# Biased attention with a feed-forward layer on one Trainium2 core: the first head pair's bias band is made on the chip, and the first eight pairs are laid in a new order

## The chip, the cores and the metric

The kernel runs on one core of a Trainium2 chip. The core has TensorE (matrix products into PSUM), VectorE, ScalarE (exponentials, copies), GpSimd and SyncE, each with an instruction queue of its own that runs in order, and 16 DMA engines that move data between HBM and SBUF. The metric is the device time of one execution in microseconds (us); less is better.

In the rows of the profile PE is TensorE, PEld its weight loads, DVE VectorE, ACT ScalarE, POOL GpSimd and SP SyncE; a "q" behind a name is that engine's instruction queue. `<-` stands between what is written and what is read, and a bracket at the end of a row gives how long the engine had been idle and what ended that. L354 is line 354 of the kernel.

## The reference

Eight batches of eight heads, 576 positions, 64 numbers a head. The bias depends on the distance of two positions through a table of 32 rows, and all distances of 128 or more share its last row.

```python
scores = scale * np.matmul(q, k.transpose(0, 1, 3, 2))        # q, k, v: (8, 8, 576, 64)
n = np.abs(pos[:, None] - pos[None, :])
bucket = np.where(n < 16, n, large)                           # large: by the logarithm of n, at most 31
scores = scores + bias_table[bucket].transpose(2, 0, 1)[None] # bias_table: (32, 8)
attn = np.exp(scores - np.max(scores, axis=-1, keepdims=True))
attn = attn / (np.sum(attn, axis=-1, keepdims=True) + 1e-09)
x = np.matmul(attn, v).transpose(0, 2, 1, 3).reshape(4608, 512)
h = x @ w_in                                                  # w_in: (512, 2048)
out = np.maximum(0.01 * h, h) @ w_out                         # w_out: (2048, 512)
```

## The kernel before, in words

**Pairs.** Two heads of a batch make a pair, one on SBUF partitions 0 to 63 and one on 64 to 127: 32 pairs, four to a batch. Keys are cut into chunks of 128, and scores are made transposed (keys on partitions, queries along the row). For pair n the steps are named by short words:

- `tq n`, `tk n`: TensorE transposes the loaded queries or keys into PSUM (line 292 up to pair 5, 288 for pairs 6 to 8; later pairs by DMA). `cq n a` or `cq n v` copies the queries to SBUF on ScalarE or VectorE (L307), `ck n` the keys on VectorE (L313), and `ap n` (L299) lays out the last 64 keys.
- `m n u`: TensorE makes score unit u. Units 0 to 3 are a chunk of 128 keys by 512 queries for both heads (L354); unit 4 is the last 64 queries of all four chunks (L347); unit 5 is the last 64 keys (L357, L358). Each takes one of two score buffers in PSUM (tag `ps_s`); unit 4 takes the banks `o0` and `o1` in the plain form and a score buffer with `s`.
- `e n u`: ScalarE takes the exponential of that unit into SBUF (L373 for units 0 to 3, L375 or L380 for unit 4, L385 for unit 5).
- `b n u`: VectorE multiplies the part of the unit near the diagonal by the bias band (L408; L401 for unit 5 of pair 0, in two halves). The bias is applied as a factor exp(bias - last bias), which is 1 at distances of 128 or more, so only a band is touched.
- `at n`, `ac n e c`: TensorE multiplies by the values and a column of ones: the last keys (L421), then chunk c for head e (L432), into banks `o0` and `o1`. `h0 n` and `h1 n` do the same in two phases with two half-height matmuls side by side (L476).
- `dv n e`: VectorE divides by the sums (L452, L454). `xt n`, `xc n`: TensorE transposes the result and VectorE copies it into `xT` (L490, L496). From pair 6 a transposing DMA does this (`xt6`), but for pair 7.

**Feed-forward.** Tokens are cut into tiles of 512. An input piece makes 128 of the 2048 hidden rows of a tile with four matmuls (L532); `l` applies the leaky function on ScalarE (L556) or, `l 1`, on VectorE (L551, L554). An output piece (`o`) has four matmuls (L584). Tile 0 can begin when all four pairs of batch 0 are in `xT` (`fin 3`); `p0` and `p1` make a piece's first three and last matmuls apart. `i m`, `i s`, `i o0`, `i o1` are input pieces in a bank of the given tag, `moe` one with its leaky function. `rows n` and `turn n` arrange later pairs for transposing DMAs (L270, L278), `sl` and `begin` issue loads.

**The order.** Pairs 0 to 7 are written out by hand in one long string `first`, a list of these steps; each step puts its instructions behind what its engines already have. From pair 8 on loops lay out the rest, and TensorE works on scores, values and feed-forward pieces by turns. `spin k` issues k products of ones whose result nobody reads (L1020): `o` in bank `o0`, `m` in a bank of the transposes.

**The bias band.** `ub` holds, for each of the eight heads on a partition of its own, the factor by signed distance in a row of 512. A band needs, on partition r, that row shifted by r. So `ub` is written to a row tensor `u_row` in HBM (L202), and `load_hk` reads it back with a stride of one element from partition to partition into `hk` (128 partitions, head, 384): the value at (r, head, x) is `u_row[head, r + x]`. `load_hk4` does the same for the last keys (L211). All are issued on SyncE's queue in this order:

```python
nc.sync.dma_start(out=udr.ap(), in_=ub)
load_hk(0, 2); load_hk(2, 4); load_hk4(0, n_pairs); load_hk(4, 6); load_hk(6, H)
```

Loads of queries, keys, values and weights are issued on GpSimd's queue (L124, L131, L137, L144, L246, L250).

## Time and profile before

| What | Value |
|---|---|
| Median of 3 runs | 365.95 us (365.65 to 367.32) |
| The profiled execution | 367.74 us, span of the profile 366.0 us |
| TensorE busy | 358.4 us (98%) |
| ScalarE busy | 244.1 us (67%) |
| VectorE busy | 189.3 us (52%) |
| First exponential of pair 0 | starts at 7.11 us |
| First band of pair 0 | starts at 12.98 us |
| First input product | starts at 32.60 us |
| First score of pair 8 | starts at 64.27 us |

A share of busy time is a mean over the span. The first 65 us, which the hand-written order covers, are unlike the rest: there the engines fill up one after another. The busy time of a matmul includes a modelled end that overlaps with the next one, so rows that group several matmuls give the better cost of one.

### The profile page before, as it was taken

The page shows a single profiled execution, that of the slowest core. Times are in us where ns is not written, and L with a number is a line of the kernel's source. Part 1 is how long each engine was busy: PE and PEld are TensorE (multiplying, and loading weights), DVE is VectorE, ACT ScalarE, POOL GpSimd, SP SyncE. Part 2 cuts the span into 40 slices and gives each one's busy share as a digit, 9 for nine tenths or more (in the row PEclk, how much of TensorE's full clock was granted, in tenths as well). Part 3 has the DMA queues.
Part 4 walks back from the last instruction along what each step waited for, and adds up shares of the span by engine and source line. Part 5 has one row for each costly group of instructions (what it writes and reads, how often), then busy time and mean ns, then how long its engine had stood idle before and what let it go on. Part 6 is the DMA issues. An engine that isn't in the chain of part 4 may idle for free.

```text
span 366.0 us, 11897 instructions
## 1 busy us (share of the span) xinstructions
PE 358.4 (98%) x5099; PEld 212.2 (58%) x5099; DVE 189.3 (52%) x499; ACT 244.1 (67%) x363; POOL 105.4 (29%) x195
## 2 busy tenths in 40 slices
PE   6999999999999999999999999999999999999996
PEld 2466555555556777686666666666666544444443
DVE  3498777877766667565666555566554300200000
ACT  5699987568957888777777777777777264055111
POOL 8867417242253433433343334211000000000000
PEclk9699999999999999999999999999999999999999
DMA  8999999999888998997997779965111000200212
GB/s 101 192 193 155 192 205 137 176 150 145 99 103 142 118 142 125 154 123 100 136 130 120 122 119 129 131 111 95 51 48 50 30 29 0 87 29 0 85 60 86
DMA packets 105851, 40.26 MB, mean 110 GB/s; under 512 B 83648, under 2 KB 101320, under 8 KB 105800
## 3 DMA queue, kind: packets, MB, share of 16 engines
q0 software_dynamic: 55200, 18.36, 48.0%
q1 hardware_dynamic: 49304, 19.06, 26.5%
q10 hardware_dynamic: 1296, 2.10, 1.6%
q8 instruction: 40, 0.66, 0.8%
q14 instruction: 11, 0.09, 0.1%
HBM read 37.68 MB, written 9.45 MB: 129 GB/s over the span
## 4 chain that ended last, share of the span: by engine, by line
PE 90%; DVE 4%; ACT 2%; DMA 1%; issue 1%; POOL 1%; ACTq 0%; POOLq 0%
PE pm L822 34%; PE pm L584 16%; PE pm L532 15%; PE ps_o L476 7%; PE ps_s L354 7%; DMA kn<-in_k_dram 1%; PE pm L718 1%; DVE at L408 1%; ACT at L373 1%; PE ps_o L421 1%; PE ps_o L442 1%; PE ps_o L432 1%; PE ps_s L822 1%; PE pm L577 1%; PE ps_s L347 1%
## 5 line engine op out<-in xcount | busy, mean ns | idle before, releaser
L373 ACT ACTIVATE at<-ps_s 128x1024 bf16<-128x1024 f32 x120 | 118.7, 1022 | 35.4 <-PE ps_s L354 34.5
L822 PE MATMUL pm<-xT,w_in_sb 64*128 64x512 bf16 x608 | 139.7, 376 | 0.0
L822 PE MATMUL pm<-w_out_sb,gt 64*128 64x512 bf16 x544 | 129.7, 376 | 0.0
L556 ACT ACTIVATE gt<-pm 128x512 bf16<-128x512 f32 x140 | 82.4, 602 | 40.0 <-PE pm L532 34.4
L408 DVE TENSOR_TENSOR at<-at,hk 128x768 bf16<-128x768 bf16 (+3 forms) x149 | 64.7, 451 | 30.8 <-ACT at L385 20.8
L822 PEld LDWEIGHTS <-w_in_sb 64*128 64x128 bf16 x608 | 51.9, 94 | 23.0 <-issue 1.2
L532 PE MATMUL pm<-xT,w_in_sb 128*128 128x512 bf16 x268 | 61.5, 379 | 0.0
L584 PE MATMUL pm<-w_out_sb,gt 128*128 128x512 bf16 x268 | 59.8, 379 | 0.0
L822 PEld LDWEIGHTS <-gt 64*128 64x128 bf16 x544 | 48.2, 94 | 19.0 <-issue 0.7
L354 PE MATMUL ps_s<-qt,kt 64*128 64x512 bf16 x240 | 45.2, 385 | 0.5 <-ACT at L373 0.2
L584 PEld LDWEIGHTS <-gt 128*128 128x128 bf16 x268 | 25.6, 98 | 30.2 <-DMA vn<-in_v_dram 0.4
L532 PEld LDWEIGHTS <-w_in_sb 128*128 128x128 bf16 x268 | 25.0, 98 | 28.1
L131 POOL DMA_DIRECT2D vn<-in_v_dram x32 | 33.6, 1054 | 9.2 <-PE pm L822 4.9
L476 PEld LDWEIGHTS <-at 64*128 64x128 bf16 x1760 | 33.8, 94 | 3.4 <-issue 0.5
L476 PE MATMUL ps_o<-vn,at 64*128 64x65 bf16 x1760 | 35.6, 190 | 0.0
L385 ACT ACTIVATE at<-ps_s 128x576 bf16<-128x576 f32 x30 | 19.7, 658 | 18.0 <-PE pm L822 18.0
L454 DVE TENSOR_TENSOR opair<-ps_o,rcp 128x320 bf16<-128x320 f32 x64 | 29.2, 487 | 1.7 <-issue 0.4
L873 DVE COPY y<-pm 128x512 f32<-128x512 f32 x17 | 11.8, 691 | 27.6 <-PE pm L822 27.6
L597 DVE COPY y<-pm 128x512 f32<-128x512 f32 x11 | 7.6, 691 | 34.1 <-PE pm L584 34.0
L1064 POOL COPY tick<-opair 1x1 bf16<-1x1 bf16 x43 | 7.8, 182 | 58.9 <-DVE opair L454 58.9
L1064 POOL COPY tick<-at 1x1 bf16<-1x1 bf16 x21 | 4.8, 227 | 58.3 <-DVE at L408 55.9
L124 POOL DMA_DIRECT2D kn<-in_k_dram x30 | 19.3, 644 | 7.0 <-issue 6.6
(106 smaller groups left out, 343.6 us busy)
## 6 DMA issues: line engine op xcount, KB each, us to landing
out_dram<-y SPq DMA_DIRECT2D x28, 256.0 KB, 3.5
qn<-in_q_dram POOLq DMA_DIRECT2D x28, 144.0 KB, 4.5
kn<-in_k_dram POOLq DMA_DIRECT2D x28, 144.0 KB, 3.8
vn<-in_v_dram POOLq DMA_DIRECT2D x24, 128.0 KB, 4.5
w_in_sb<-in_moe_w_in_dram POOLq DMA_DIRECT2D x4, 512.0 KB, 8.7
w_out_sb<-in_moe_w_out_dram POOLq DMA_DIRECT2D x2, 1024.0 KB, 14.1
...
```

Source lines behind the costliest of these rows:

```text
L124: nc.gpsimd.dma_start(out=dst[0:RQ, h0:h1, :, :].rearrange("r h c d -> r h (c d)"), in_=src[b, h0:h1, :, :].rearrange("h (r c) d -> r h (c ...
L131: nc.gpsimd.dma_start(out=vn[b % NBUF][:, c, h0:h1, 0:D], in_=v[b, h0:h1, c * P : (c + 1) * P, :].rearrange("h s d -> s h d"),)
L354: nc.tensor.matmul(ps[:, e, :], lhsT=kt[r, u * P : (u + 1) * P], rhs=qt[r, 0:512], start=True, stop=True)
L373: nc.scalar.activation(at[:, :, u, 0:512], ps, AF.Exp, scale=scale)
L385: nc.scalar.activation(at4[:, 0:w], ps.rearrange("p e i -> p (e i)")[:, 0:w], AF.Exp, scale=scale)
L408: nc.vector.tensor_tensor(out=o, in0=o, in1=m, op=ALU.mult)
L454: nc.vector.tensor_tensor(out=opair[:, 0:m, e * D : (e + 1) * D], in0=ps[:, :, 0:D], in1=rcp.to_broadcast([P, m, D]), op=ALU.mult)
L476: m = nc.tensor.matmul(outs[n][e][:, ic * (D + 1) : (ic + 1) * (D + 1)], lhsT=at[halves[r], o : o + P], rhs=vn[b % NBUF][halves[r], c, 2 * ...
L532: nc.tensor.matmul(pm, lhsT=w_in_sb[:, c, f * P : (f + 1) * P], rhs=xT[c][:, T * TT : (T + 1) * TT], start=(c == 0), stop=(c == n_cc - 1))
L556: nc.scalar.activation(g, pm, AF.Prelu, bias=0.0, scale=1.0, alpha=0.01)
L584: nc.tensor.matmul(pm, lhsT=gt[:, f, ts * P : (ts + 1) * P], rhs=w_out_sb[:, f, :], start=(f == 0), stop=(f == n_fc - 1))
L822: m = nc.tensor.matmul(o, lhsT=w, rhs=x, start=was is None, stop=need[bank] == 0)
```

## The change

The band of heads 0 and 1 is no longer read from `u_row`; `load_hk(0, 2)` goes, while `u_row` and the other reads stay. In its place:

- `place`, a row of zeros with two ones for each head, made on VectorE, gives one-hot weights. `dm` (`windows`) is 12 products that put 12 windows of `ub`, each 159 long and 32 apart, of both heads on 24 partitions of one PSUM bank. `dc` (`windows_copy`) copies them to SBUF as `wins` on ScalarE.
- `hm` (`slants`) is 32 transposes: number j takes columns j to j + 127 of `wins` (24 x 128) and writes 24 columns of 128 partitions, so that each partition gets its shift. `hc e` (`slants_copy`) copies head e's 384 columns into `hk` on VectorE, putting window i, shift j at column 32 i + j.

The string `first` is laid anew. Ten of 17 spins go (9, 2, 3 and 3 become one group of 7). `m 0 1` comes ahead of `tq 1`; `m 0 4` and `m 3 4` use `o0` and `o1`, `m 1 4` a score buffer; pair 3's values go in two halves; `cq 5` and `cq 6` go to VectorE and `cq 7` to ScalarE; bands, values and feed-forward pieces of pairs 0 to 7 stand in another order. There are as many input (16) and output (4) pieces as before. The step `ii` is defined and not used.

```diff
--- before.py
+++ after.py
@@ -206,6 +206,37 @@
             in_=bass.AP(tensor=udr, offset=h0 * UW, ap=[[1, P], [UW, h1 - h0], [1, BW]]),
         )
 
+    NB0 = BW // 32
+    place = per.tile([H, 2 * NB0 + NB0 - 1], BF16, name="place")
+    nc.vector.memset(place, 0.0)
+    for e in range(2):
+        c = e * NB0 + NB0 - 1
+        nc.vector.tensor_copy(out=place[:, c : c + 1], in_=ident[0:H, e : e + 1])
+    wins = per.tile([2 * NB0, 32 + P], BF16, name="wins")
+    near = {}
+
+    def windows():
+        near["w"] = ps_o_pool.tile([P, 512], FP32, name="ps_d", tag="o1")
+        for i in range(NB0):
+            nc.tensor.matmul(near["w"][0 : 2 * NB0, 0 : 31 + P],
+                             lhsT=place[:, NB0 - 1 - i : 3 * NB0 - 1 - i], rhs=ub[:, 32 * i : 32 * i + 31 + P],
+                             start=(i == 0), stop=(i == NB0 - 1))
+
+    def windows_copy(eng):
+        copy = nc.scalar.copy if eng == "a" else nc.vector.tensor_copy
+        copy(out=wins[:, 0 : 31 + P], in_=near.pop("w")[0 : 2 * NB0, 0 : 31 + P])
+
+    def slants():
+        near["h"] = ps_o_pool.tile([P, 8 * P], BF16, name="ps_h", tag="o1")
+        for j in range(32):
+            nc.tensor.transpose(near["h"][:, j * 2 * NB0 : (j + 1) * 2 * NB0], in_=wins[:, j : j + P],
+                                identity=ident[0 : 2 * NB0, 0 : 2 * NB0])
+
+    def slants_copy(e, eng):
+        copy = nc.scalar.copy if eng == "a" else nc.vector.tensor_copy
+        copy(out=hk[:, e, :].rearrange("p (i j) -> p j i", j=32),
+             in_=near["h"][:, 0 : 64 * NB0].rearrange("p (j e i) -> p e j i", e=2, i=NB0)[:, e])
+
     def load_hk4(p0, p1):
         for e in range(2):
             nc.sync.dma_start(
@@ -214,7 +245,6 @@
                             ap=[[1, SL], [2 * UW, p1 - p0], [1, P + SL]]),
             )
 
-    load_hk(0, 2)
     load_hk(2, 4)
     load_hk4(0, n_pairs)
     load_hk(4, 6)
@@ -1089,35 +1119,35 @@
         exp(n, u, qk_mm(n, u))
 
     first = """
-        spin 9 o, tq 0, cq 0 a, tk 0, ck 0, ap 0, spin 2 o,
-        begin 0, m 0 0, m 0 2, tk 1, tq 1, e 0 0, m 0 1, ck 1, e 0 2, m 0 5, e 0 1, e 0 5, m 0 4 s, m 0 3,
-        e 0 4, spin 3 m, cq 1 v, ap 1, e 0 3, m 1 0, tk 2, b 0 5, ck 2, b 0 1, e 1 0, m 1 1, ap 2, m 1 2,
-        e 1 1, b 0 0, b 0 4, m 1 4, tq 2,
-        begin 1, e 1 4, spin 3 m, m 1 3, b 0 2, e 1 2, b 1 0, cq 2 v, at 0, ac 0 1 0, ac 0 1 1, ac 0 0 0,
-        b 1 1, ac 0 1 2, m 1 5, e 1 3, ac 0 1 3, ac 0 0 1, e 1 5, ac 0 0 2, ac 0 0 3, m 2 0, e 2 0, tk 3,
-        b 1 4, dv 0 0, m 2 1, b 1 5, tq 3, e 2 1, dv 0 1, m 2 3, ck 3, at 1, e 2 3, ac 1 0 0, m 2 2, b 1 2,
-        cq 3 v,
-        begin 2, ac 1 0 1, ac 1 1 0, m 2 5, ac 1 1 1, b 2 0, ac 1 1 2, e 2 2, ac 1 1 3, ac 1 0 2, ac 1 0 3,
-        e 2 5, ap 3, b 2 1, m 3 0, dv 1 0, xt 0, m 2 4 s, b 2 5, xc 0, e 3 0, dv 1 1, tk 4, m 3 2, e 2 4,
-        m 3 1, ck 4, b 2 4,
-        begin 3, at 2, e 3 2, ac 2 0 0, b 2 2, ac 2 0 1, ac 2 1 0, e 3 1, xt 1, b 3 0, m 3 3, tq 4,
-        ac 2 0 2, xc 1, ac 2 0 3, dv 2 0, ac 2 1 1, ac 2 1 2, e 3 3, ac 2 1 3, m 3 5, dv 2 1, cq 4 a,
-        e 3 5, ap 4, tq 5, m 3 4 s, xt 2, m 4 0, e 3 4, b 3 1, e 4 0, m 4 1, e 4 1, b 3 5,
-        begin 4, b 3 4, at 3, ac 3 1 0, ac 3 0 0, b 3 2, xc 2, ac 3 0 1, cq 5 a, ac 3 1 1, ac 3 0 2,
-        ac 3 0 3, ac 3 1 2, fin 3, ac 3 1 3, p0 0, m 4 2, e 4 2, m 4 3, dv 3 0.1, b 4 1, e 4 3, xt 3 o0,
-        p0 1, xc 3, b 4 0, p1 0 0, m 4 4 s, p1 1 0, m 4 5, tk 5, rows 6, e 4 5, e 4 4, moe, ck 5, b 4 5,
-        ap 5, moe, tq 6, m 5 0, b 4 4, cq 6 a, at 4, m 5 1, e 5 1, ac 4 1 0, ac 4 1 1, ac 4 0 0, ac 4 0 1,
-        begin 5, e 5 0, b 4 2, ac 4 0 2, ac 4 0 3, ac 4 1 2, dv 4 0, tk 6, ac 4 1 3, m 5 5, e 5 5, dv 4 1,
-        sl 5 1, i m, m 5 2, ck 6, b 5 0, l 0, m 5 3, b 5 1, m 5 4, i m, e 5 2, e 5 3, xt 4, i s, l 1,
-        rows 7, e 5 4, xc 4, i s, b 5 5, l 0, sl 5 2, b 5 4,
-        begin 6, i m, at 5, ap 6, l 0, b 5 2, m 6 0, l 0, m 6 1, tk 7, ac 5 0 0, ac 5 1 0, ck 7, ac 5 1 1,
-        ac 5 0 1, ac 5 0 2, ac 5 0 3, ac 5 1 2, tq 7, e 6 1, e 6 0, dv 5 0, ac 5 1 3, dv 5 1, sl 6 1, i s,
-        l 0, m 6 2, xt 5, m 6 3, e 6 2, cq 7 v, b 6 0, e 6 3, xc 5, m 6 4, ap 7, i m, m 6 5, e 6 4, i m,
-        l 0, l 1, i o0, i m, e 6 5, m 7 0, m 7 1, l 0, b 6 5, b 6 1, sl 6 2, at 6, l 0, b 6 2, b 6 4,
-        begin 7, rows 8, ac 6 1 0, ac 6 1 1, e 7 0, ac 6 0 0, ac 6 0 1, ac 6 0 2, e 7 1, ac 6 1 2,
-        ac 6 0 3, ac 6 1 3, tk 8, dv 6 0, dv 6 1, sl 7 1, ck 8, i s, i m, l 0, m 7 4, l 0, m 7 2, xt6,
-        m 7 3, b 7 0, e 7 4, o, e 7 3, turn 7, b 7 1, o, e 7 2, b 7 4, m 7 5, tq 8, cq 8 a, b 7 2, o,
-        e 7 5, b 7 5, ap 8, sl 7 2, o,
+        spin 7 o, tq 0, tk 0, ck 0, cq 0 a,
+        begin 0, ap 0, dm, m 0 0, m 0 2, dc a, hm, hc 0 v, tk 1, hc 1 v, e 0 0, e 0 2, m 0 1, e 0 1, tq 1,
+        ck 1, m 0 5, m 0 4, cq 1 v, e 0 5, e 0 4, m 0 3, tk 2, e 0 3, ck 2, ap 1, m 1 4 s, tq 2, b 0 1,
+        e 1 4, m 1 0, b 0 2, e 1 0, m 1 1,
+        begin 1, b 0 4, e 1 1, b 0 5, m 1 2, ap 2, m 1 3, cq 2 v, b 0 0, e 1 2, at 0, e 1 3, ac 0 1 0,
+        b 1 0, ac 0 1 1, ac 0 0 0, m 1 5, b 1 2, ac 0 0 1, e 1 5, ac 0 0 2, ac 0 1 2, ac 0 1 3, b 1 1,
+        ac 0 0 3, m 2 0, m 2 1, dv 0 0, e 2 0, tk 3, m 2 3, b 1 5, b 1 4, dv 0 1, tq 3, at 1, ck 3,
+        ac 1 0 0, e 2 1, m 2 5, ac 1 0 1,
+        begin 2, ac 1 1 0, b 2 1, ac 1 1 1, e 2 3, ap 3, m 2 2, cq 3 v, ac 1 1 2, e 2 5, ac 1 1 3, e 2 2,
+        b 2 5, ac 1 0 2, ac 1 0 3, b 2 0, dv 1 0, m 3 0, dv 1 1, xt 0, e 3 0, xc 0, m 2 4 s, tk 4, m 3 2,
+        e 2 4,
+        begin 3, b 2 2, at 2, b 2 4, m 3 1, xt 1, ac 2 0 0, ac 2 0 1, ck 4, ac 2 1 0, e 3 2, e 3 1, b 3 2,
+        ac 2 0 2, m 3 3, ac 2 1 1, xc 1, ap 4, ac 2 0 3, tq 4, ac 2 1 2, dv 2 0, e 3 3, cq 4 a, ac 2 1 3,
+        dv 2 1, m 3 5, e 3 5, tq 5, m 3 4, b 3 1, e 3 4, m 4 1, xt 2, b 3 5, at 3, m 4 0, b 3 0, e 4 1,
+        e 4 0,
+        begin 4, b 3 4, cq 5 v, xc 2, fin 3, b 4 0, h0 3, m 4 2, e 4 2, h1 3, m 4 3, e 4 3, dv 3 0.1, p0 0,
+        m 4 4 s, xt 3 o0, b 4 1, p0 1, xc 3, m 4 5, rows 6, p1 0 0, p1 1 0, i o0, e 4 5, tk 5, ck 5, i m,
+        ap 5, l 0, e 4 4, b 4 5, tq 6, m 5 1, m 5 0, at 4, b 4 2, b 4 4, ac 4 1 0, cq 6 v, l 0,
+        begin 5, ac 4 0 0, ac 4 0 1, ac 4 0 2, ac 4 0 3, e 5 0, ac 4 1 1, dv 4 0, tk 6, ac 4 1 2, e 5 1,
+        ac 4 1 3, m 5 5, e 5 5, dv 4 1, i m, l 0, m 5 2, m 5 3, e 5 2, ck 6, m 5 4, sl 5 1, e 5 4, e 5 3,
+        i m, b 5 5, l 0, xt 4, b 5 0, ap 6, rows 7, xc 4, i s, b 5 2, i o1, i m, sl 5 2, m 6 1, b 5 4, l 0,
+        begin 6, m 6 0, b 5 1, l 0, l 0, at 5, ac 5 0 0, e 6 1, ac 5 0 1, tk 7, e 6 0, ac 5 1 0, ac 5 0 2,
+        tq 7, cq 7 a, ac 5 0 3, ac 5 1 1, ac 5 1 2, dv 5 0, ac 5 1 3, dv 5 1, sl 6 1, i s, l 0, m 6 2,
+        ck 7, ap 7, b 6 1, m 6 4, xt 5, m 6 3, e 6 2, xc 5, i m, e 6 3, m 6 5, e 6 4, e 6 5, i m, b 6 2,
+        i o0, l 1, b 6 5, i m, b 6 4, m 7 1, b 6 0, l 0, at 6, m 7 0, rows 8, sl 6 2, l 0,
+        begin 7, l 0, e 7 0, ac 6 1 0, ac 6 0 0, ac 6 0 1, ac 6 0 2, b 7 0, ac 6 1 1, tk 8, i m, ac 6 0 3,
+        ac 6 1 2, ac 6 1 3, e 7 1, ck 8, i m, m 7 2, dv 6 0, l 0, e 7 2, m 7 3, dv 6 1, m 7 4, l 1, ap 8,
+        sl 7 1, e 7 3, o, turn 7, b 7 1, b 7 2, m 7 5, e 7 5, e 7 4, o, b 7 4, o, b 7 5, sl 7 2, tq 8,
+        cq 8 a, xt6, o,
     """
 
     def word(w):
@@ -1159,6 +1189,23 @@
             if f == 0: gts[T] = gt_pool.tile([P, n_fc, TT], BF16, name="gt")
             in_steps(pm, T, f, range(n_cc))
             open_.append((T, f, pm))
+        elif k == "dm": windows()
+        elif k == "dc": windows_copy(a[0])
+        elif k == "hm": slants()
+        elif k == "hc": slants_copy(a[0], a[1])
...
         elif k == "l": leaky(*open_.pop(0), a[0])
         elif k == "o": piece_out()
         else: raise ValueError(k)
```

13 lines of the change are left out of this document (added).

## The prediction, written before the result was known

> **What bounds the kernel now.** I read the shares of the page first, then the busy time by stretches, then the timeline of the first 37 us row by row, then the landing times of single transfers.
>
> ```profile
> PE 358.4 (98%) x5099; PEld 212.2 (58%) x5099; DVE 189.3 (52%) x499; ACT 244.1 (67%) x363; POOL 105.4 (29%) x195
> ...
> 20.00:25.00 5.00, 4.83 (x91) 3.09 (x89) 4.89 (x14) 4.78 (x7) 2.84 (x6) 1.00 1.65 187
> 25.00:30.00 5.00, 4.72 (x117) 3.46 (x115) 4.56 (x14) 4.96 (x7) 2.67 (x4) 1.00 1.59 186
> ...
> 35.00:40.00 5.00, 4.86 (x66) 2.71 (x66) 3.03 (x8) 4.66 (x9) 2.98 (x5) 1.00 1.38 189
> ...
> 100.00:200.00 100.00, 100.00 (x1854) 69.09 (x1852) 63.35 (x166) 76.47 (x110) 39.12 (x76) 1.00 0.91 126
> ```
>
> TensorE is busy 98% of the span and all of 100 to 200 us, so from some point on a microsecond is worth a microsecond of TensorE work. The change can gain only where TensorE is not yet full. Between 20 and 30 us TensorE looks busy too (4.83 and 4.72 of 5), but a matmul's busy time holds its modelled end; ScalarE (4.78, 4.96) and VectorE (4.89, 4.56) are what is full there. So there is a first stage, set by exponentials and bands, and a second, set by TensorE. These rows give both ends of the first:
>
> ```profile
> 6.14 0.61 PE L1020 MATMUL ps_w<-const-bfloat16-1.0 128*128 128x512 bf16 x2
> 7.11 1.94 ACT L373 ACTIVATE at<-ps_s 128x1024 bf16<-128x1024 f32 x2 [1.03 <-PE ps_s L354]
> 8.34 0.92 SPq L204 DMA_DIRECT2D hk<-u_row  x2
> 9.23 0.50 PEld L292 LDWEIGHTS <-kn 96*64 96x64 bf16 x12 [2.00 <-DMA kn<-in_k_dram]
> 9.95 0.76 DVE L313 COPY kt<-ps_t 128x576 bf16<-128x576 bf16 x1 [2.62 <-PE ps_t L292]
> 10.97 1.02 ACT L373 ACTIVATE at<-ps_s 128x1024 bf16<-128x1024 f32 x1 [1.93 <-PE ps_s L354]
> 12.98 0.52 DVE L401 TENSOR_TENSOR at<-at,hk 64x192 bf16<-64x192 bf16 x2 [1.48 <-DMA hk<-u_row]
> 13.13 1.46 PE L1020 MATMUL ps_w<-const-bfloat16-1.0 128*128 128x512 bf16 x3
> 13.24 1.02 ACT L373 ACTIVATE at<-ps_s 128x1024 bf16<-128x1024 f32 x1 [0.16 <-PE ps_s L354]
> 15.18 2.15 ACT L373 ACTIVATE at<-ps_s 128x1024 bf16<-128x1024 f32 x2 [0.92 <-PE ps_s L354]
> 15.81 0.76 DVE L313 COPY gt<-ps_t 128x576 bf16<-128x576 bf16 x1 [2.31 <-PE ps_t L292]
> ...
> 20.31 3.77 ACT L373 ACTIVATE gt<-ps_s 128x1024 bf16<-128x1024 f32 x4
> ...
> 30.18 0.60 ACT L375 ACTIVATE at<-ps_s 128x512 bf16<-128x512 f32 x1
> 30.28 1.59 DVE L408 TENSOR_TENSOR at<-at,hk 128x768 bf16<-128x768 bf16 x4
> 31.36 1.40 PE L432 MATMUL ps_o<-vn,at 128*128 128x65 bf16 x40
> 32.60 0.81 PE L532 MATMUL pm<-xT,w_in_sb 128*128 128x512 bf16 x3
> ...
> 36.30 0.45 PE L292 MATMUL ps_t<-ident,kn 96*64 96x96 bf16 x12
> 36.79 1.89 PE L532 MATMUL pm<-xT,w_in_sb 128*128 128x512 bf16 x8
> 64.27 0.39 PE L354 MATMUL ps_s<-qt,kt 64*128 64x512 bf16 x2
> ```
>
> ```profile
> 31.27 0.15 PE ps_o L421 x10
> ...
> 44.23 2.59 PE pm L532 x12
> ```
>
> The first exponential (`e 0 0`) starts at 7.11, the last of pair 3 (`e 3 4`) ends at 30.18 + 0.60 = 30.78. From 20.31 on ScalarE has no gap worth counting; before that it idles 1.93 + 0.16 + 0.92 = 3.01 us, each time for scores. The first of these, 1.93, is `m 0 1`, which stands behind `tk 1` and `tq 1` in TensorE's order, and `tk 1` waits for pair 1's keys (the row at 9.23, 2.00 idle, released by that transfer). The bias band is waited for once, 1.48 us, by VectorE at 12.98; then VectorE waits 2.31 us more for `tk 2`, which stands behind three spins and a score. The input product starts at 32.60. `tk 5` starts at 36.30, and pair 8's first score at 64.27.
>
> After 36.30 the work of TensorE up to 64.27 is, by the order: 14 input and 4 output pieces of 4 matmuls (0.86 each: the two rows are of the chain of waits, 2.59 for 12 matmuls and 0.15 for a pair's tails), 3 pairs of values with tails (1.4 + 0.15), 12 scores at 0.22, six smaller ones 1.15, 5 transposed halves and `xt` twice, 1.9: 15.5 + 4.6 + 2.6 + 1.2 + 1.9 = 25.8 of 28.0 us. So 2.2 us are stalls; the rest only moves with its start.
>
> **The change part by part.** *Spins.* Ten of 17 go (0.43 to 0.2 us each). All stood where TensorE had nothing else ready, and no work waits on their result: 0, except that the clock may miss them (rival B).
>
> ```profile
> 17.23 0.65 ACT L380 ACTIVATE at<-ps_q 128x256 bf16<-128x256 f32 x2
> ...
> DMA to landing us min/median/max: 4.5/4.5/4.5
> ...
> L476 PE MATMUL ps_o<-vn,at 64*128 64x65 bf16 x1760 | 35.6, 190 | 0.0
> L385 ACT ACTIVATE at<-ps_s 128x576 bf16<-128x576 f32 x30 | 19.7, 658 | 18.0 <-PE pm L822 18.0
> ```
>
> These are a copy of 2 x 256 columns, the time to landing of the band's read issued at 8.34, and the page's groups of the small matmuls on values and of the narrow exponentials (mean ns last before the bar).
>
> *The products (`dm`) and their copy (`dc`).* Twelve products of 159 columns and 8 rows stand before `m 0 0`, where two spins of 512 columns stood (6.14). Nothing like them is in the trace. Lower bound: the 65-column matmuls of 31.36, 1.40 / 40 = 0.035 each, 0.4 us. Upper: a full spin, 0.61 / 2, 3.7 us. I take the spin scaled by columns, 0.22 x 159 / 512 = 0.067, so 0.8 us, because 159 columns is nearer to the narrow rows; against the two spins' 0.43 that is 0.37 later. `dc` reads 24 x 159 on ScalarE ahead of `e 0 0`; the first row gives 0.65 / 2 for 256 columns, so at most 0.33, and it runs while `m 0 0` runs. Bounds 0 and 0.33; I take 0. `e 0 0` then starts near 7.45: cost 0.35.
>
> *The transposes (`hm`).* 32, each a weight load of 128 columns and 24 moving columns. Lower bound 0.035 each as at 31.36: 1.1 us. Upper bound the 0.19 us that its group has as one matmul's whole duration, if nothing overlaps: 6.1 us. I take 1.1: weight loads of the same width, narrower moving side. They fit between `m 0 2` (ended about 7.5) and 9.2, where pair 1's keys land, so TensorE's idle 1.7 us covers them. Without that cover they would cost their 1.1 us in full. The new wait: `hm` waits for `dc`, and behind it in TensorE's queue stand `tk 1` and `m 0 1`.
>
> *The two copies (`hc`) on VectorE.* 128 x 384 from PSUM with a stride each; the copy at 9.95 takes 0.76 for 576 columns, so 0.5 each (bounds 0.4 and 0.76). VectorE idles 2.62 us until 9.95. `hm` ends near 8.6, so the copies end at 9.65; `ck 1` is ready at the same time. Cost 0, and each further tenth delays `ck 1`, `cq 1` and pair 1. `place` (a memset and two one-column copies) falls in VectorE's pause before the first key copy: 0.
>
> *The band through HBM.* Of six reads of `u_row`, the first (192 KB) goes; the write and the other five stay. SyncE's queue reaches pair 1's read about 0.5 us sooner. Pair 1's keys were issued ahead of all this and keep their 9.2. The gain is on VectorE: pair 0's band is in SBUF at 9.65 instead of 8.34 + 4.5 = 12.8.
>
> *The new order, first stage.* `m 0 1` stands right behind `tk 1`: keys at 9.2, transposes 0.3 and scores 0.4 later, so `e 0 1` at 9.95 instead of 10.97. From there I walked the three queues with two score banks: `e 0 5` 10.95 (0.66 by its group), `e 0 4` (now in two halves, +0.05) 11.6, `e 0 3` 12.25, `e 1 4` 13.2, `e 1 0` 13.8, then every 0.95 up to `e 1 3`, `e 1 5` to 18.25. ScalarE idles 0.5 before `e 0 1`, 0.2 before `e 2 0`, and I allow 0.3 elsewhere: 1.0 instead of 3.01. `e 3 4` ends at 30.78 + 0.35 + 0.05 - 2.0 = 29.2. VectorE must keep up: from its band at 16.60 in the old order to the last of pair 3 at 30.28 + 1.59 = 31.87 it is busy nearly throughout, 15.3 us. The same work plus the two half bands of pair 0 (0.5) begins at 12.6 in the new order (`tk 2` no longer waits behind spins), so 28.4 without gaps; I find one of 0.5 for `e 1 2` and others together as long, 29.4, and the last band follows `e 3 4` at 29.2 + 0.45. Bands end about 29.7, 2.1 us ahead.
>
> Transfers have to be there too. The tightest are the keys of pair 3 (issued first here), pair 4 and pair 8, each with the largest time to landing:
>
> ```profile
> 11.23 0.64 POOL L124 DMA_DIRECT2D kn<-in_k_dram  x1 [0.30 <-DMA kn<-in_k_dram]
> DMA to landing us min/median/max: 7.8/7.8/7.8
> ...
> 12.54 0.67 POOL L124 DMA_DIRECT2D kn<-in_k_dram  x1
> DMA to landing us min/median/max: 8.7/9.3/9.9
> ...
> 39.45 0.67 POOL L124 DMA_DIRECT2D kn<-in_k_dram  x1
> DMA to landing us min/median/max: 11.1/12.2/13.3
> ```
>
> 11.23 + 7.8 = 19.0, where `tk 3` comes at 18.7; 12.54 + 9.9 = 22.4, needed at 23.5; and 39.45 + 13.3 = 52.75 for `rows 8`, which stood after 56: slack for a lead of 3 us. Cost 0, with the 0.3 at `tk 3` hidden behind `e 2 0`.
>
> ```profile
> 64.66 0.78 PE L476 MATMUL ps_o<-vn,at 64*128 64x65 bf16 x40
> ```
>
> *Values of pair 3 in halves* (`h0`, `h1`): 80 matmuls, by this row 2 x 0.6, its end left out, against 1.35 at 31.36: gain 0.1. `m 4 2` and `m 4 3` (0.44) now stand ahead of the input product, where TensorE would have waited for bands.
>
> *Second stage.* ScalarE loses `cq 5` and `cq 6` and takes `cq 7`; VectorE the reverse, 0.7 us each, with 3.03 of 5 busy there: hidden; if VectorE were full it would cost 0.7. By my walk the first-stage work plus `m 4 5` and the second input piece ends at 34.5; in the old order at 36.3, where `tk 5` follows it. The lead is 1.8. Then an input piece follows at once, where before TensorE went from `tk 5` at 36.30 to the next piece at 36.79, 0.2 more than the transposes need: 0.3 more of lead with the gap ahead of `tk 5`. The later order has the same 25.8 us of work; which of its 2.2 us of stalls stay I cannot tell, so 0, between -0.7 and +0.7. `xt6`, a transposing transfer, goes behind pair 9's on SyncE's queue instead of ahead of it; its rows are wanted only with pair 7's: 0.
>
> **Sum:** +0.35 (products) +0.05 (two halves) -2.0 (ScalarE's idle) -0.4 (`cq 5` off ScalarE, halves, earlier scores) -0.3 (piece behind `tk 5`) +0.2 (VectorE's gaps) = -2.1. The profiled execution took 367.74, span 366.0 and 1.7 round it; it would be 365.6. The runs' median, 365.95, is 1.8 below that execution: 363.85, say 363.9.
>
> **The rivals.** *A, the forecast:* 363.9, by itself 362.6 to 364.8 (stall term, and ScalarE's idle between 0.7 and 1.5). Chance 0.58.
>
> ```profile
> 9.00:10.00 1.00, 0.77 (x20) 0.77 (x22) 0.05 (x1) 0.05 (x1) 0.78 (x2) 0.64 2.00 139
> 10.00:11.00 1.00, 1.00 (x13) 0.44 (x10) 1.00 (x2) 0.03 (x1) 0.86 (x2) 0.50 1.16 117
> ...
> 16.00:17.00 1.00, 1.00 (x24) 0.59 (x21) 0.97 (x2) 0.89 (x2) 0.65 (x1) 0.95 1.26 248
> ```
>
> *B, the clock falls and costs part of it.* The granted clock was 0.64 at 9 to 10 us, 0.50 until 16, 0.95 in 16 to 17. It fell after 1.7 idle us, and came back after spins that now are gone. For: the 32 transposes use 24 of 128 rows, and may count for little. Against: by the durations above TensorE is occupied in 2.3 of the 3.1 us from 6.1 to 9.2. At the low clock scores for `e 0 1` come 0.5 later, and if it lasts to pair 0's values (1.4 us) half of that again is lost: 0.5 to 1.5, so 364.9. [...] Chance 0.16.
>
> *C, the change doesn't do what it says:* the band was hidden anyway. For: only VectorE waited for it, 1.48 us, and 2.31 us for `tk 2` right after. Then the order alone decides, and if VectorE's gaps in pairs 1 to 3 are 2 us instead of 1, and stalls after 36 grow by 0.7, 0.3 is left: 365.6. Chance 0.16.
>
> *D, slower:* the transposes do not overlap, 0.19 us each. `hm` then ends at 7.5 + 6.1 = 13.6 with `tk 1` and `m 0 1` behind it, so `e 0 1` starts 4.4 later than in A: 363.9 + 4.4 = 368.3. It decides from 0.115 us a transpose (1.7 of cover + 2.0 of lead, over 32). For: they read their windows at odd offsets, as no load in the trace does. Against: 40 loads as wide took 1.40. Chance 0.10.
>
> **How the numbers follow.** 0.5% is 1.8 us, about what a measurement of this kernel can tell. A gives faster with 0.47 and within with 0.11; B and C within; D slower, 0.10. So faster 0.47, same 0.43, slower 0.10. The range 362.6 to 366.3 takes in A, B and C and leaves out D and the edges.
>
> **What the profile after would show.** Right: `e 0 1` near 10, pair 0's first band near 12.6, `e 3 4` ending near 29.2, the input product near 31.5, pair 8's first score near 62. `hm` taking over 1.7 us, a clock of 0.5 past 13 us, or VectorE idle over 1.5 us in 13 to 30, would show the step that failed. A lead at 34 us that is gone at pair 8 would put it on the later order.

## The result: 0.7% slower

The changed kernel takes 368.01 us (367.84 to 369.85, 7 runs) against 365.93 for the kernel before in the same session, a ratio of 1.0068, 95% interval 1.0046 to 1.0089: 2.1 us slower, where the prediction had 363.9 and 362.6 to 366.3. Executions of one kernel differ by up to 1.2% here (a_warm below: 366.13 to 370.41), and the three profiles of the kernel before differ in their clock (at half rate for 10.2, 6.8 and 3.4 us in executions of 368.8, 367.74 and 366.43), so each profile below stands beside its own execution's time. Those of the changed kernel make two groups, 367.8 to 368.1 and 369.2 to 369.9 (six and eight of the 14 in two sessions). So the 2.1 us are the loss of the first group; the median of the second session is 369.2, and the loss of the second group about 3.3. The first profile of the changed kernel is of one of 369.35 us; another, of 368.07 and so of the first group, is read here (a_again below). Its timeline (start, duration, engine, line, operation, and in brackets the idle time before it and what ended it):

```profile
4.77 0.45 PE L322 MATMUL ps_t<-ident,qn 96*64 96x96 bf16 x12 [0.98 <-DMA qn<-in_q_dram]
5.54 0.45 PE L322 MATMUL ps_t<-ident,kn 96*64 96x96 bf16 x12 [0.33 <-DMA kn<-in_k_dram]
5.92 1.00 PE L221 MATMUL ps_d<-ub,place 8*24 8x159 bf16 x12
6.95 0.28 ACT L227 CAST wins<-ps_d 24x159 bf16<-24x159 f32 x1 [1.06 <-PE ps_d L221]
7.46 1.94 ACT L403 ACTIVATE at<-ps_s 128x1024 bf16<-128x1024 f32 x2 [0.22 <-PE ps_s L384]
7.78 1.03 PE L232 MATMUL ps_h<-ident,wins 24*128 24x24 bf16 x32
8.85 3.50 DVE L237 COPY hk<-ps_h 128x384 bf16<-128x384 bf16 x2 [1.74 <-PE ps_h L232]
10.02 1.02 ACT L403 ACTIVATE at<-ps_s 128x1024 bf16<-128x1024 f32 x1 [0.62 <-PE ps_s L384]
11.99 0.94 DVE L343 COPY kt<-ps_t 128x576 bf16<-128x576 bf16 x1
12.41 0.39 PE L377 MATMUL ps_q<-qt,kt 64*128 64x64 bf16 x7 [1.05 <-DVE hk L237]
21.27 2.86 ACT L403 ACTIVATE gt<-ps_s 128x1024 bf16<-128x1024 f32 x3 [0.90 <-PE ps_s L384]
34.29 0.82 PE L562 MATMUL pm<-xT,w_in_sb 128*128 128x512 bf16 x2
64.61 0.39 PE L384 MATMUL ps_s<-qt,kt 64*128 64x512 bf16 x2
```

TensorE is still busy 97% of the span (356.8 us), against 98% before. `dm` (L221) took 1.00, `dc` (L227) 0.28, `hm` (L232) 1.03, the first exponential (L403) starts at 7.46, `e 0 1` at 10.02: all near the forecast. The two band copies (L237) took 3.50 us, 1.75 each. They hold PSUM bank `o1`, so `m 0 4` (L377) waits for them (TensorE 1.05 us, the row at 12.41), and `ck 1` (L343) stands behind them until 11.99. Pair 2's first exponential is at 21.27, the first input product (L562) at 34.29, pair 8's first score (L384) at 64.61.

The kernel before, profiled again in an execution of 366.43 us (b_again2), near its median:

```profile
6.77 2.96 ACT L373 ACTIVATE at<-ps_s 128x1024 bf16<-128x1024 f32 x3 [1.03 <-PE ps_s L354]
7.65 0.45 PE L292 MATMUL ps_t<-ident,kn 96*64 96x96 bf16 x12 [0.47 <-DMA kn<-in_k_dram]
12.36 0.52 DVE L401 TENSOR_TENSOR at<-at,hk 64x192 bf16<-64x192 bf16 x2 [2.67 <-DMA hk<-u_row]
13.23 0.76 DVE L313 COPY gt<-ps_t 128x576 bf16<-128x576 bf16 x1 [0.35 <-PE ps_t L292]
17.96 1.02 ACT L373 ACTIVATE gt<-ps_s 128x1024 bf16<-128x1024 f32 x1 [0.24 <-PE ps_s L354]
30.73 0.81 PE L532 MATMUL pm<-xT,w_in_sb 128*128 128x512 bf16 x2
62.41 0.39 PE L354 MATMUL ps_s<-qt,kt 64*128 64x512 bf16 x2
```

Pair 8's first score (L354 in this kernel's lines) is at 62.41, not at the 64.27 of the profile that the prediction read. The three first exponentials run without a gap from 6.77: pair 1's keys were there at 7.65, not at 9.23, and the 1.93 us in which ScalarE waited for them do not exist. The changed kernel is 64.61 - 62.41 = 2.2 us behind at this point, where the measured loss is 2.1 and these two executions differ by 1.6. From there on the two spans have 302.3 (before) and 301.7 us left. So the whole loss of this execution is made before pair 8.

One place where it can be made is the granted clock. Columns of the next two are the stretch (us), its length and TensorE's busy time (matmuls), the granted clock, the share of the DMA engines and GB/s; first the changed kernel (a_again), then before (b_again2):

```profile
5.50:7.00 1.50, 1.46 (x26) 0.98 1.07 153
7.00:8.90 1.90, 1.90 (x40) 0.50 1.38 179
8.90:12.30 3.40, 2.45 (x29) 0.50 1.39 144
12.30:16.00 3.70, 3.36 (x45) 0.50 1.35 188
16.00:20.00 4.00, 3.24 (x41) 0.50 1.36 212
```

```profile
5.50:7.00 1.50, 1.44 (x18) 1.00 1.24 173
7.00:8.90 1.90, 1.34 (x29) 1.00 1.33 171
8.90:12.30 3.40, 2.31 (x16) 0.78 1.32 168
12.30:16.00 3.70, 3.70 (x55) 0.75 1.36 208
```

TensorE of the changed kernel was occupied for all but 0.04 us of 5.5 to 8.9, but it was at half rate from 6.9 until 20.6 us. Ahead of that, behind its seven spins, it had stood 0.98 and 0.33 us for loads (the rows at 4.77 and 5.54). Before fell for 3.4 us only, around 12. In the first profile (369.35) the clock came up as late as 23.3 us by the trace's clock record, and pair 8's first score is at 65.87, 1.26 later than above: the two groups. The column reads 1.00 ahead of its first record there, so the clock has to be read from the pace (`dm` took 1.77 us there, 1.00 above):

```profile
6.00 1.77 PE L221 MATMUL ps_d<-ub,place 8*24 8x159 bf16 x12
65.87 0.39 PE L384 MATMUL ps_s<-qt,kt 64*128 64x512 bf16 x2
```

### The profile page after: what moved, and what is told of

It is laid out like the page before. It is cut to its first block, busy times and chain, and to the rows that moved or that the text cites. A ratio compares the mean times of both kernels' runs of the same rounds, so it can differ in the third digit from the quotient of the medians.

```text
span 367.6 us, 12051 instructions
## 1 busy us (share of the span) xinstructions
PE 360.4 (98%) x5173; PEld 207.2 (56%) x5173; DVE 193.5 (53%) x505; ACT 243.8 (66%) x364; POOL 105.4 (29%) x195
## 4 chain that ended last, share of the span: by engine, by line
PE 94%; ACT 2%; DVE 2%; DMA 1%; issue 0%; ACTq 0%; POOLq 0%
PE pm L852 34%; PE pm L614 16%; PE pm L562 16%; PE ps_s L384 8%; PE ps_o L506 7%; PE ps_o L462 2%; PE pm L748 1%; PE ps_o L451 1%; ACT at L403 1%; PE ps_o L472 1%; PE ps_s L852 1%; PE ps_t L322 1%; DVE hk L237 1%; DMA qn<-in_q_dram 1%; PE ps_s L377 1%; PE pm L607 1%
## 5 line engine op out<-in xcount | busy, mean ns | idle before, releaser
L403 ACT ACTIVATE at<-ps_s 128x1024 bf16<-128x1024 f32 x120 | 118.3, 1023 | 32.5 <-PE ps_s L384 32.3
L562 PE MATMUL pm<-xT,w_in_sb 128*128 128x512 bf16 x268 | 61.7, 380 | 0.0
L384 PE MATMUL ps_s<-qt,kt 64*128 64x512 bf16 x240 | 45.6, 393 | 1.2 <-ACT at L403 1.2
L562 PEld LDWEIGHTS <-w_in_sb 128*128 128x128 bf16 x268 | 24.8, 98 | 28.2 <-issue 0.5
L506 PE MATMUL ps_o<-vn,at 64*128 64x65 bf16 x1840 | 36.7, 190 | 0.0
L415 ACT ACTIVATE at<-ps_s 128x576 bf16<-128x576 f32 x30 | 19.7, 655 | 18.7 <-PE pm L852 17.9
L124 POOL DMA_DIRECT2D kn<-in_k_dram x30 | 19.4, 648 | 7.0 <-issue 7.0
```

The costliest lines, as they stand in the source:

```text
L124: nc.gpsimd.dma_start(out=dst[0:RQ, h0:h1, :, :].rearrange("r h c d -> r h (c d)"), in_=src[b, h0:h1, :, :].rearrange("h (r c) d -> r h (c ...
L384: nc.tensor.matmul(ps[:, e, :], lhsT=kt[r, u * P : (u + 1) * P], rhs=qt[r, 0:512], start=True, stop=True)
L403: nc.scalar.activation(at[:, :, u, 0:512], ps, AF.Exp, scale=scale)
L415: nc.scalar.activation(at4[:, 0:w], ps.rearrange("p e i -> p (e i)")[:, 0:w], AF.Exp, scale=scale)
L506: m = nc.tensor.matmul(outs[n][e][:, ic * (D + 1) : (ic + 1) * (D + 1)], lhsT=at[halves[r], o : o + P], rhs=vn[b % NBUF][halves[r], c, 2 * ...
L562: nc.tensor.matmul(pm, lhsT=w_in_sb[:, c, f * P : (f + 1) * P], rhs=xT[c][:, T * TT : (T + 1) * TT], start=(c == 0), stop=(c == n_cc - 1))
```

## The experiments

The theory after the result had two parts: the change took away spins, which costs clock; and it copies the band with a slow pattern, which costs 1.25 us a copy. The rival was that the new order, or making the band on the chip, is itself the loss. Every ratio is against the kernel before, with its 95% interval. In the labels a stands for the changed kernel and b for the kernel before.

**Copies alone (a_copy).**

```
-  copy(out=hk[:, e, :].rearrange("p (i j) -> p j i", j=32), in_=...rearrange("p (j e i) -> p e j i", ...)[:, e])
+  copy(out=hk[:, e, :].rearrange("p (i j) -> p i j", j=32), in_=...rearrange("p (j e i) -> p e i j", ...)[:, e])
```

> The changed kernel with the two band copies written in running order (32 shifts inside, 12 windows outside), nothing else. Theory copies (each copy takes 1.75 us instead of 0.5, VectorE and the bank o1 are held 2.5 us too long, and this is what cost the time): each copy falls to about 0.5 us, the second key copy starts near 10.5 instead of 12.9, and the time falls by 1.5 to 2.5 from 368.0, to 365.5 to 366.5. Theory clock (TensorE at half rate up to 23 us is what cost the time): the copies get short, but values and scores of pairs 0 and 1 stay at half rate, e 2 0 comes by at most 1 us sooner, 367.0 to 367.8. Theory late order (pairs 4 to 7): no change, 368.0.

368.27 us, 1.0059 [1.0037, 1.0081]. The copies fell to 0.51 each, and the median stands where the two sessions of the changed kernel have theirs (368.01 and 369.2), so what the copies cost by themselves can't be read from it.

```profile
9.78 1.02 DVE L237 COPY hk<-ps_h 128x384 bf16<-128x384 bf16 x2 [2.55 <-PE ps_h L232]
64.09 0.39 PE L384 MATMUL ps_s<-qt,kt 64*128 64x512 bf16 x2
```

This is an execution of 367.9 us. Its pair 8 comes 1.8 us earlier than in the first profile of the changed kernel (65.87), but its clock also came up earlier, at 19.7 us instead of 23.3, and the rows do not part the two.

**Spins alone (a_spin).** As before: nine at the start, three behind `m 0 3`, three ahead of `m 1 3`.

```
-  spin 7 o, tq 0, ...                  ...  m 0 3, tk 2,           ...  ap 2, m 1 3,
+  spin 9 o, tq 0, ...                  ...  m 0 3, spin 3 m, tk 2, ...  ap 2, spin 3 m, m 1 3,
```

> The changed kernel with 8 of the ten spins put back: 9 at the start, 3 behind m 0 3 and 3 ahead of m 1 3; the copies as they are. Theory clock: the clock rises before 17 us instead of 23, the 25 value products of pair 0 take 0.9 us instead of 1.6, e 2 0 starts near 21 instead of 22.5, the time falls by 1 to 2 to 366.0 to 367.0. Theory copies: spins stand in waits and change nothing or cost up to 0.5, 368.0 to 368.5. Theory late order: 368.0.

370.81 us, 1.0137 [1.0112, 1.0162]: worse than without them. Four of its five executions had a mean clock of 0.98, as the first group of the changed kernel. The profile is of the fifth (368.75 us): TensorE was busy 1.55 of the 3.4 us from 8.9 to 12.3, with the slow copies to wait for, its clock was 0.60 there and 0.50 up to 16, and the first three later spins took 1.46 us. If all six ran at that rate in the other four, an estimate from this row is 2.9 us, about what the kernel lost; no profile of one of these four shows it.

**Both (a_both).**

> Both edits. If copies and clock each cost what their theory says, the two gains add to 3 or 4 us, 364.0 to 365.0, below the kernel before. If only one of them counts, the time is that of the single edit. Theory late order: 368.0, and the lead at the first input product is lost by pair 8.

367.39 us, 1.0021 [1.0003, 1.0038]; the profile is of an execution of 366.42.

```profile
8.29 1.02 DVE L237 COPY hk<-ps_h 128x384 bf16<-128x384 bf16 x2 [1.26 <-PE ps_h L232]
10.90 1.45 PE L1050 MATMUL ps_w<-const-bfloat16-1.0 128*128 128x512 bf16 x3
62.41 0.39 PE L384 MATMUL ps_s<-qt,kt 64*128 64x512 bf16 x2
```

```profile
5.50:7.00 1.50, 1.50 (x28) 1.00 1.22 169
7.00:8.90 1.90, 1.90 (x50) 0.97 1.26 166
8.90:12.30 3.40, 3.40 (x31) 0.52 1.33 145
```

So with the spins there the copies are worth 370.81 - 367.39 = 3.4 us, and with cheap copies these spins are worth 368.27 - 367.39 = 0.9. The gains do not add as was expected (364 to 365). Pair 8's first score is where before has it. The clock still fell for one stretch, nearly all of 8.9 to 12.3 us (0.52), behind 3.4 us in which TensorE had no gap.

**The kernel before with the changed kernel's spins (b_nospin).** Seven at the start, the other ten out.

```
-  spin 9 o, ... ap 0, spin 2 o, begin 0, ... e 0 4, spin 3 m, cq 1 v, ... e 1 4, spin 3 m, m 1 3,
+  spin 7 o, ... ap 0,           begin 0, ... e 0 4,           cq 1 v, ... e 1 4,           m 1 3,
```

> The kernel before with ten of its 17 spins taken out (7 at the start, none later), nothing else. Theory clock: the rise at 16 us moves to 20 us or later, and the time grows by 1 to 2 to 367.0 to 368.0. Theory copies, and the prediction's own step (spins cost nothing and bring nothing): 365.5 to 366.2, no change.

367.92 us, 1.0043 [1.0031, 1.0056]; pair 8's first score at 63.59 in an execution of 367.63, whose clock came up at 19.4 us. Ten spins that produce nothing are worth 2.0 us. With equal spins and cheap copies the changed kernel (368.27) is no faster than this.

**Before, again (b_again, b_again2).** The same kernel, for other profiles.

> The kernel before, its instructions unchanged, for a second profile of it. Its profiled execution of before took 367.74 us, 1.8 above the median, with a clock of 0.991 (a fall to half from 9.4 to 16.2 us). Theory: that execution was not the ordinary one, and the prediction worked out a gain on stalls that most executions do not have. An ordinary one then takes 365.9, has pair 8's first score at about 62.1 instead of 64.27, pair 2's first exponential near 18.5 instead of 20.31, a clock of 0.995 or more, and ScalarE idle well below 3.0 us ahead of that exponential. Rival: pair 8's first score is at 64.3 again in an execution of 365.9, and what differed lay behind it or outside of the span.

366.2 us, 1.0011 [0.9989, 1.0033]. The profile is of an execution of 368.8 (clock 0.986, pair 8's first score at 65.20), which settled nothing; so it was repeated.

> The kernel before, unchanged, for another profile of it. Theory (the prediction's base was not ordinary): an execution of 365.3 to 366.4 us has pair 8's first score at 61.9 to 62.5 and pair 2's first exponential at 17.5 to 18.5, as before's neighbours with two spins fewer or four more have (62.19 and 62.27; 17.98 and 17.68). Rival: it is at about 64.3 in such an execution too, and the rest of the span is shorter by 2 us.

366.2 us, 1.0 [0.9975, 1.0026]; the rows are shown above: 366.43, 62.41 and 17.96. The theory holds and the rival falls.

**The band on the chip in the old order (b_chip).** Cheap copies, all 17 spins.

```
-  begin 0, m 0 0, m 0 2, tk 1, tq 1, e 0 0,
+  begin 0, dm, m 0 0, m 0 2, dc a, hm, hc 0 v, hc 1 v, tk 1, tq 1, e 0 0,
```

> The order and the 17 spins of before; only the band of pair 0 is made on the chip (dm, dc, hm, and both hc with copies in running order ahead of tk 1), and its read from HBM is dropped. Theory: the wait for the band (1.48 us on VectorE) is followed at once by the wait for pair 2's transposes, so its end is worth nothing, and the 0.8 us of dm, 1.0 of hm and 1.0 of the copies are covered by the wait for pair 1's keys but for the 0.4 us that dm puts ahead of the first scores: 366.0 to 366.6 against 365.9, pair 8's first score 62.2 to 62.8. Rival (the band's wait did hold pair 0 back): 364.5 to 365.2.

369.51 us, 1.01 [1.0076, 1.0124]: a miss of three microseconds, and not for the reason that either theory had. Pair 8's first score is at 62.21, where before has 62.41: early or late, the band moves next to nothing there. What is lost lies behind it, 303.9 us to the end of the span against 302.3. The timeline, a stretch, and TensorE's waits (for what, us in total, times, longest) in an execution of 368.23:

```profile
62.21 0.39 PE L384 MATMUL ps_s<-qt,kt 64*128 64x512 bf16 x2
...
100.00:150.00 50.00, 49.09 (x886) 33.34 (x880) 32.70 (x85) 38.58 (x55) 20.07 (x40) 1.00 1.03 128
...
PE ps_o L506 <- issue: 0.9, 1, 0.9
PE pm L852 <- issue: 0.8, 1, 0.8
```

TensorE was busy 49.09 of the 50 us from 100 to 150. Two pauses of 0.9 and 0.8 us stand among rows of equal matmuls, with nothing that the trace shows as awaited. Before's profiles have none as long (0.2 us in b_again2), a_warm2 below has one of 0.7. Why they are there stays open; so does the 1.3 us by which its median is above this execution.

**The new order without the band on the chip (a_hbm).** Spins of 9, 2, 3 and 3; `load_hk(0, 2)` back, and `dm`, `dc`, `hm`, `hc` out.

> The new order with 9, 3 and 3 spins as before has them (and 2 where dm stood), and the band of pair 0 read from HBM as before; dm, dc, hm and hc are left out. It is the order alone. With both, and the same spins, 367.39. Theory: the order gives nothing over that of before; without the work for the band at the start 366.0 to 367.0, and pair 8's first score at 62.0 to 62.9, since VectorE waits about 0.5 us for the band at 12.5 but has 1.0 us of copies less. Rival 1 (the new order needs the early band, as it was laid round it): over 368, with VectorE waiting over 1.5 us for the band. Rival 2 (the order is what gains and the band what costs): 364 to 365.

368.16 us, 1.0056 [1.0039, 1.0073]; its pair 8 stands at 62.01, the earliest of all, and it loses that and more behind it:

```profile
62.01 0.39 PE L354 MATMUL ps_s<-qt,kt 64*128 64x512 bf16 x2
69.60 0.65 DVE L319 COPY qt<-tu 128x576 bf16<-128x576 bf16 x1 [4.12 <-DMA tu<-pr]
73.60 0.33 PE L421 MATMUL ps_o<-v,at 64*128 64x65 bf16 x10 [1.20 <-DVE xT L515]
```

A transposing transfer for a later pair landed late here (VectorE idle 4.12 us for it), and after that TensorE stood 1.20 us for a copy on VectorE. VectorE waited 0.88 us for the band, where the theory had 0.5 and rival 1 over 1.5. Rival 1 had the time, but not for its reason, and no price of the theories can be read from this kernel's time; what can be read is 62.01: up to pair 8 the order alone gains 0.4 us at most (62.41 in b_again2, 62.19 and 62.27 in before's two neighbours below).

**Before with four spins more (b_warm).** Between `m 0 2` and `tk 1`.

```
-  m 0 2, tk 1, tq 1,
+  m 0 2, spin 4 o, tk 1, tq 1,
```

> The kernel before with four more spins (0.86 us at full clock) between m 0 2 and tk 1, where TensorE waits for pair 1's keys from about 7.4 to 9.2 in the profiled execution. Theory: they keep the clock from falling at 9.4, which a part of the executions shows: the median 365.3 to 365.8 and none with a clock under 0.995; if ordinary executions do not have that fall anyway, 365.9 as before. Rival: the keys come earlier in ordinary executions, the spins delay tk 1 by up to 0.9 us, and the time is 366.3 to 366.8.

365.9 us, 1.0003 [0.9987, 1.002]; pair 8's first score at 62.27 in an execution of 366.09. No change that can be measured: this execution kept its clock (0.999) and is where before's ordinary ones are. One of the twelve still had 0.991, which the theory had ruled out.

**Which spins (b_seven, b_nolate).** Before with seven at the start and the other eight kept, and before with nine and the other eight out.

> The kernel before with 7 spins at the start instead of 9; its other eight (2, 3 and 3) stay. With 7 at the start and the other eight gone it took 367.92. Theory (the first spins decide whether the clock comes up before the first scores): TensorE works at half rate up to at least 9 us, the first exponential at about 8.0 instead of 7.0, pair 8's first score at 62.8 to 63.4, 366.6 to 367.5. Rival (the eight later ones are what holds the clock): 365.9, as before.

367.01 us, 1.0028 [1.0007, 1.0049]: its executions spread from 365.66 to 369.64, and the profile is of the shortest:

```profile
9.07 0.61 PE L354 MATMUL ps_s<-qt,kt 64*128 64x512 bf16 x2
```

Two of these matmuls take 0.39 us at the full clock (8.28 in b_again2) and 0.61 at a granted 0.50 (16.45 in a_again). So TensorE was at half rate beyond 9 us, as the theory had it, and yet pair 8's first score is at 62.19: half rate so early cost nothing that shows there. The four executions with a mean clock of 0.986 took 367.5 to 369.6 us; none of them was profiled.

> The kernel before with its 9 spins at the start and without the eight later ones (2, 3 and 3). Theory (two steps, the clock must be brought up and then held): the clock is full by 6 us, falls between 9 and 10 and comes back by 16 to 20; pair 8's first score at 63.5 to 64.5 and 367.3 to 368.3. Rival (once it is up, the scores and exponentials hold it): 365.5 to 365.9, since the eight spins took TensorE's time.

368.19 us, 1.0047 [1.0024, 1.0069]; the eight later spins are worth 2.2 us. (Two at the start are worth 1.1 by b_seven, and all ten 2.0 by b_nospin: the parts do not add.) TensorE and ScalarE while waiting for pair 1's keys, in an execution of 368.55:

```profile
9.53 0.69 PE L292 MATMUL ps_t<-ident,kn 96*64 96x96 bf16 x12 [2.16 <-DMA kn<-in_k_dram]
11.28 1.02 ACT L373 ACTIVATE at<-ps_s 128x1024 bf16<-128x1024 f32 x1 [2.46 <-PE ps_s L354]
64.26 0.39 PE L354 MATMUL ps_s<-qt,kt 64*128 64x512 bf16 x2
```

**The changed kernel, mended (a_start, a_warm).** Cheap copies and nine spins at the start; and in a_warm three and three later, and four between `m 0 2` and `hm`, where TensorE waits for `dc`:

```
-  dm, m 0 0, m 0 2, dc a, hm,
+  dm, m 0 0, m 0 2, dc a, spin 4 o, hm,
```

> The changed kernel with both band copies in running order, and 9 spins at the start instead of 7; none later. With 7 it took 368.27, with 9, 3 and 3 367.39. Theory: the start alone gives a full clock up to 8.9 us and then a fall that lasts to 16 or later: 367.5 to 368.5, pair 8's first score at 63.0 to 64.0. Rival (the start is all of the difference): 367.2 to 367.5.

367.54 us, 1.0036 [1.0013, 1.006], the first score of pair 8 at 64.09 in an execution of just that time. The full clock up to 8.9 us that the theory had did not show: `dm` took 1.77 us, as in the first profile of the changed kernel, and the clock came up at 19.9 us. Nine spins at the start did not bring it up here.

> The changed kernel with both band copies in running order, spins of 9, 3 and 3, and four more spins (0.86 us at full clock) between m 0 2 and hm, where TensorE waits for the copy dc. In the same kernel without these four TensorE was occupied without a gap from 5 to 9 us, and its clock still fell at 8.88, behind 3.4 us with only 0.6 us of products other than transposes and those of the 8-row operands. Theory (such work does not hold the clock): the four spins keep it from falling, pair 8's first score comes at 61.9 to 62.4, 366.0 to 367.2. Rival (the clock falls whatever TensorE does): it falls at 8.9 again, the spins delay hm and tk 1 by 0.5 to 0.8 us, and the time is 367.6 to 368.2.

366.75 us, 1.0033 [1.0005, 1.0061]. Seven of twelve executions took 366.1 to 366.8, three over 369.5, and the profile is of one of those (370.41, half rate until 16.4 us, first score of pair 8 at 66.13). So the changed kernel and this one were profiled again.

> The changed kernel, unchanged, for another profile of it; the first took 369.35 with its clock at half rate until 23.3 us. Theory: an execution of 367.8 to 368.1 has pair 8's first score at 64.2 to 64.6 instead of 65.87, with a shorter stretch of half rate before 25 us and the same two copies of 1.75 us. Rival: it is at 65.9 again, and the later stages differ.

369.2 us, 1.0069 [1.0045, 1.0093]; its profile (368.07) is the one that is read under the result: 64.61, the theory's side, though 0.01 above its bound.

> The changed kernel with cheap copies, spins of 9, 3 and 3, and four more ahead of hm, unchanged, for another profile; the first took 370.41 with half rate until 16.4 us. Theory: an execution of 366.1 to 366.8 has the clock full from about 5.5 us on without a fall at 8.9, and pair 8's first score at 62.2 to 62.8: the mended kernel with a full clock is where before is, or up to 0.6 us behind. Rival 1 (the new order gains once the clock holds): pair 8's first score at 60.5 to 61.5, and the loss lies behind it. Rival 2: the clock falls at 8.9 here too.

366.88 us, 1.0011 [0.9993, 1.0028]. Profile of an execution of 366.89:

```profile
7.33 1.94 ACT L403 ACTIVATE at<-ps_s 128x1024 bf16<-128x1024 f32 x2
8.41 0.95 PE L232 MATMUL ps_h<-ident,wins 24*128 24x24 bf16 x32
9.41 1.02 DVE L237 COPY hk<-ps_h 128x384 bf16<-128x384 bf16 x2 [2.24 <-PE ps_h L232]
32.14 0.82 PE L562 MATMUL pm<-xT,w_in_sb 128*128 128x512 bf16 x2
62.46 0.39 PE L384 MATMUL ps_s<-qt,kt 64*128 64x512 bf16 x2
```

```profile
5.50:7.00 1.50, 1.40 (x26) 1.00 1.20 174
7.00:8.90 1.90, 1.84 (x26) 1.00 1.32 168
8.90:12.30 3.40, 3.18 (x61) 1.00 1.29 138
```

With the four spins the clock was 1.00 where it fell to 0.52 in a_both; all eight executions here had a mean clock of 0.999 or 1.00, ten of a_both's twelve 0.99 to 0.995. Pair 8's first score is at 62.46, before's at 62.41: with its clock and its copies mended, the change neither gains nor loses there. From 368.27 (a_copy) to 366.75 and 366.88 the spins, with four more than before had behind its first scores, are worth 1.4 to 1.5 us in this order (before stood at 365.9 to 366.1 in every session). The two medians are still 0.8 and 0.9 above before's, the first with an interval that lies just above 1, the second with one that includes it; what is behind this stays open. No version beats the kernel before.

## Why the prediction was wrong

**The base (the step of the sum).** The prediction worked out -2.1 us against the profiled execution, 365.6, and then took the same 2.1 from the median, 365.95, as if the stalls that it removed were in every execution. The largest term, -2.0 for ScalarE's idle 3.01 us, was the mark of that execution: its keys came at 9.23 and its clock fell until 16. In b_again2 the first two of those gaps, 1.93 and 0.16, are gone, and pair 2's first exponential starts at 17.96 instead of 20.31. The prediction saw that the execution was 1.8 us above the median and did not ask where these 1.8 us were. They were ahead of pair 8 (64.27 against 62.41), in the same stalls: in b_again2 ScalarE idles 0.83 + 0.24 = 1.07 us up to pair 2, as much as the prediction left to the new order (1.0). The read execution was no rare one, but not the ordinary one either: of 114 executions of the kernel before in the later sessions, 27 had a mean clock of 0.991, as it had, or less, and they took 367.3 us in the median, the other 87 took 365.9.

**Spins at 0.** "No work waits on their result" was true, and the price was still wrong: 2.0 us in the old order (2.2 for the later eight alone), and in the new one with cheap copies 0.9, or 1.4 to 1.5 with four more ahead of `hm`. In the new order with the slow copies, putting eight back cost 2.8. What the profiles show beside the price is the clock: where they are out it came up at 19.4 us or later (b_nospin, a_copy, the first profile) or was down from 6.9 to 20.6 (a_again).

**`hc` at 0.5 each, bounds 0.4 to 0.76.** Measured 1.75 where the copy writes each row with a stride of 64 bytes; written in running order and read with a stride, it takes 0.51 (a_copy). The row it was sized by (0.76 for 576 columns) wrote in order. The prediction named what then follows (`ck 1` and pair 1 late) but not that the bank keeps `m 0 4` waiting. What the error cost by itself is not settled (a_copy); with the spins back it was 3.4 us (a_spin against a_both). How the loss of 2.1 us divides between copies and clock is thus not known; that both together make what was lost ahead of pair 8 is what a_warm2 shows (62.46).

**Rival B** (the clock falls, 364.9) had the clock right, and was given 0.16. That `hm`'s transposes may count for little was a supposition ahead of the runs. It agrees with a_both, granted 0.52 in 8.9 to 12.3 us behind 3.4 us of gapless work that was mostly transposes and 8-row products, and with a_warm2, granted 1.00 with full-width spins among the same work. But b_chip had nearly the same work without a gap from 5.5 to 8.9 us, with two spins ahead of `dm`, and kept 1.00 in its profile (five of its six executions had a mean of 0.989 to 0.995), and a_again's fall at 6.9 also has idle time ahead of it (0.98 and 0.33 us). So these runs bear it out in part, and do not show it to be the cause. Of the signs of failure that the prediction named, the clock of 0.50 past 13 us is the one that showed (a_again). The price of 0.5 to 1.5 holds the 0.9 to 1.5 measured in this order, but it was added to a forecast whose base was not ordinary.

**Rival C** (the band was hidden anyway) was right in that, though not in its time, 365.6: with the band early and the old order, pair 8 starts at 62.21, with the band late at 62.41 and 62.27. In b_again2 VectorE waits 2.67 us for the band and then still 0.35 for `tk 2`.

**Rival D** gave 368.3, close to the result by luck, and is refuted: `hm` took 0.95 to 1.04, 0.03 us each, not 0.19.

**Right:** `dm` 1.00 for 0.8 at a full clock; `dc` 0.28, hidden; `hm` 1.0 for 1.1; the first exponential at 7.46 for 7.45; `e 0 1` at 10.02 for 9.95, by luck, with earlier keys and a lower clock; the later order, which was given 0 within 0.7. From `tk 5` to pair 8's first score the old order takes 28.0 us, in the profile that the prediction read (36.30 to 64.27) and in b_again2 (34.44 to 62.41); the new one, with one input piece (0.86) that it puts ahead of `tk 5`, takes 27.5 (37.96 to 64.61 in a_again, 35.81 to 62.46 in a_warm2). Of these 0.5 us less, 0.3 were forecast. And where clock and copies are mended (a_warm2) the walk of the new order was within 0.7 in three of its signs: `e 3 4` ended at 29.87 for 29.2, the input product came at 32.14 for 31.5, pair 8's first score at 62.46 for 62. The first band was 1.0 late, at 13.56 for 12.6. It was before's ordinary execution that stood there too.
